# The first two-chunk group's hidden layer in 26 products, its weight sums by accumulating transfers, and block decays made on chip

## The chip, the cores and the metric

The kernel runs on one core of one Trainium2 chip. The metric is the device time of one execution in microseconds (us). Three runs of the kernel before gave 662.61, 662.81 and 662.85; their median, 662.81, is the time that a change is held against. The engines are TensorE (PE, with its weight loads shown apart as PEld), VectorE (DVE), ScalarE (ACT), GpSimd (POOL) and SyncE (SP, which here only issues transfers).

## The reference

Two blocks follow each other: a retention layer with decay, and a two-layer network with the gate h * erf(softplus(h)).

```python
# q, k, v: batch 4, 8 heads, 768 positions, 64 wide, float32
state = gamma[None, :, None, None] * state + np.einsum('bhd,bhe->bhde', k[:, :, t], v[:, :, t])
y[:, :, t] = scale * np.einsum('bhd,bhde->bhe', q[:, :, t], state)
...
x = attn_out.transpose(0, 2, 1, 3).reshape(B * S, H * D)      # 3072 tokens x 512
h = x @ w_in                                                  # w_in 512 x 2048, float64 as given
sp = np.maximum(h, 0.0) + np.log1p(np.exp(-np.abs(h)))
out = ((h * erf(sp)) @ w_out).astype(np.float32)              # w_out 2048 x 512, float64 as given
```

## The kernel before

The sequence is worked through in 24 pieces of 128 positions (`j`), the network in groups (`g`). The first 512 tokens are done plainly: groups 0 to 3 are four quarters of the hidden width (`hidden`, L860 and L878), each followed by the gate on ACT (`gate`, L817 and L830: softplus and erf over 128x2048) and a product with DVE (`gated`, L849), and by the second layer `project` (L896), which sums in four PSUM banks `o0` to `o3` over all four groups. From group 4 on (named `G0`) a group is 256 tokens by half of the hidden width, `s` = (g - G0) % 2 telling which half. There `hidden_steps` computes the layer with 26 block products instead of 32: `STEPS` lists for each product the combined weight block, the combined input block, one of four PSUM banks, and into which blocks of `h` the result is added or subtracted. A first addition to a block of `h` is a copy on ACT (L965, L967), all later ones are additions on DVE (L963). The combined inputs come from `x_sums` (18 DVE subtractions and additions of 128x128, L933), the combined weights from 30 sums of 128x256 blocks of `w_in_sb`, `W_SUMS`, by `sum_in` (L344 on DVE). The second layer of these groups is `project_part` (L1034), seven products instead of eight; three of them stand in the stream of the next group's `hidden_steps`, behind steps 14, 18 and 24. Its combined weights, T1 to T4 for each half, are made by `sums`: a negating copy on ACT (L352) and an accumulating transfer inside the on-chip memory issued by POOL (L353).

The order of instructions on every engine is the order in which the program writes them; no scheduler moves them. An engine that waits holds all that is queued behind it. `waiting`, `pace` and `need` only choose where the weight conversions are written among the other work. The weights come as 64-bit floats and are made 32-bit in 16 pieces by five DVE operations (L313 to L331) and one on ACT (L314) each; `place` says which of four spare areas a piece is loaded into, and `load_pieces_after` loads a later piece when an earlier one in the same area is used up.

Before the change the first half-width group, G0, doesn't use `STEPS`: its weight blocks are not yet summed. `hidden_plain` (L980, copies L983) does its 32 products of 128x128 by 128x256, in two runs with `sub_begin` (scores of the next piece of the sequence) between them. On DVE, in the order of the program, stand around it: `sum_in(1, 12)`, `prepared(j)` (scaling and transposing the next piece, L537 to L550), `gated(3)`, `sum_in(1, 20)`, `x_sums(G0)`, and the rest of the sums of half 1; the sums of half 0 follow before and inside group G0+1. Half 1 is summed first since group G0 + 1 needs it first.

At the very start PE runs `keep_warm` (L495, products of the identity matrix, each two instructions) until the first scaled keys are there (`ret_scale`, L514) and can be transposed (`ret_transpose`, L524). The decay factors of the keys in the layout of the later pieces, `kq_b` and `by_b`, are loaded by SP during group 2 in 17 small transfers (`load_block_scales`, L469 and L473); `block_scales` (L476 to L480) makes the other factors of them on DVE and POOL.

Of the kernel before, what the change touches and what calls it, by code (L numbers as in the profile page):

```python
# [19 lines left out]
P = 128  # L20
C = 128
TCH = 512
FG = 4
# [23 lines left out]
    (16, 2, 6, "+"),  # L47
    (17, 8, 10, "-"),
    (4, 4, 17, "+"),
    (10, 10, 16, "+"),  # L50
    (18, 16, 4, "-"),
# [3 lines left out]
    (21, 9, 20, "+"),  # L55
# [4 lines left out]
    (24, 20, 12, "-"),  # L60
    (25, 18, 7, "+"),
    (2, 2, 3, "+"),
    (8, 12, 8, "-"),
    (12, 17, 12, "-"),
# [3 lines left out]
    (16, 16, 7, "+"),  # L68
# [7 lines left out]
    (13, 13, 7, "-"),  # L76
)
# [28 lines left out]
    (24, (0, 1), 1, False, ((7, False),)),  # L106
    (25, 15, 2, False, ((2, True),)),
# [4 lines left out]
    (17, 1, 3, True, ((2, False), (4, True))),  # L112
# [7 lines left out]
    (16, 12, 1, False, ((3, True),)),  # L120
# [16 lines left out]
def kernel(  # L137
# [87 lines left out]
    def w_in_of(ft, kk):  # L225
        half, s, i = ft // (2 * FG), ft % (2 * FG) // FG, ft % FG
        return w_in_sb[:, s, 4 * (2 * half + i // 2) + kk, i % 2 * P : (i % 2 + 1) * P]

    def w_out_of(ft):
        half, s, i = ft // (2 * FG), ft % (2 * FG) // FG, ft % FG  # L230
        return w_out_sb[:, s, 2 * half : 2 * half + 2, i, :]
# [14 lines left out]
    last_power = halves(spare[1][:, :CE])  # L246
# [7 lines left out]
    place = [n % 4 if n < n_p - 4 else (n - n_p + 4) % 3 for n in range(n_p)]  # L254
# [30 lines left out]
    def conversion(n):  # L285
# [4 lines left out]
        half, s, at = i // 4, i % 4 // 2, i % 2  # L290
# [49 lines left out]
    def sum_in(s, upto):  # L340

        assert all(("hidden", 2 * FG + s * FG + u) in done for u in range(FG))
        for to, a, b, sign in W_SUMS[in_sums[s] : upto]:
            nc.vector.tensor_tensor(w_in_sb[:, s, to], w_in_sb[:, s, a], w_in_sb[:, s, b], op=OP[sign])  # L344
        in_sums[s] = max(in_sums[s], upto)

    def sums(s):

        assert ("project", s) in done
        x = {name: w_out_sb[:, s, at] for name, at in OUT.items()}  # L350
        for to, a, b in (("T1", "12", "11"), ("T2", "22", "T1"), ("T3", "22", "12"), ("T4", "21", "T2")):
            nc.scalar.activation(x[to], x[b], AF.Copy, scale=-1.0)  # L352
            nc.gpsimd.dma_start(x[to], x[a], accum_op=ALU.add)  # L353
            done.add((to, s))
            yield
# [47 lines left out]
    nc.scalar.copy(idle_out, ident[:, :1])  # L403

# [60 lines left out]
    def load_block_scales():  # L465
        for s, d in itertools.product(range(2), range(2)):
            part = slice((2 * s + d) * 32, (2 * s + d + 1) * 32)
            for u in range(HP):
                nc.sync.dma_start(  # L469
                    kq_b[part, 0, 0, u],  # L470
                    decay_k[:, 2 * u + s : 2 * u + s + 1].rearrange("(a p) h -> p (a h)", p=32),
                )
        nc.sync.dma_start(by_b[:, 1], decay_s)  # L473
# [13 lines left out]

    psum_turn = itertools.cycle((ps_r, ps_h))
# [8 lines left out]
    keep_warm(7)  # L497
# [68 lines left out]
    def ret_mask(j):  # L566
        AM[j] = ret.tile([P, 2, HP, C], F32, name="am")
        for s in range(2):
            nc.vector.tensor_tensor(
                AM[j][:, s], SC[j][s], causal[:, None, :].to_broadcast([P, HP, C]), op=ALU.mult  # L570
            )
        pace(-1.2)
# [59 lines left out]
    def sub_mask(j):  # L632
        AM[j] = ret.tile([P, 2, HP, C], F32, name="am")
        for s in range(2):
            nc.vector.tensor_tensor(
                AM[j][:, s, :, :D],
                SC[j][s][:, :, :D],
                causal_d[:, None, :].to_broadcast([P, HP, D]),
                op=ALU.mult,
            )  # L640
# [26 lines left out]
    def sub_results(j):  # L667
# [15 lines left out]
        for crossed in range(2):  # L683
            for u in PAIRS:
                for a in range(2):
                    r = 1 - a if crossed else a
                    col, t = u // 2, slice(a * D, (a + 1) * D)
                    own = slice(col * D, (col + 1) * D)
                    nc.tensor.matmul(
                        pp[a][own, 2 + u % 2, :D] if crossed else pp[a][own, u % 2, t],  # L690
                        V[j][t, 2 * u + r, :],
                        AM[j][t, r, u, :D],
                        start=False, stop=True, skip_group_check=True,
                    )
# [18 lines left out]
    def sub_visit(j, g):  # L713
# [31 lines left out]
        def of_values(crossed):  # L745
            for u in PAIRS:
                for a in range(2):
                    r = 1 - a if crossed else a
                    col, t = u // 2, slice(a * D, (a + 1) * D)
                    own = slice(col * D, (col + 1) * D)  # L750
                    nc.tensor.matmul(  # L751
                        other[a][own, u % 2, D:] if crossed else pp[a][own, u % 2, t],
                        V[j][t, 2 * u + r, :],
                        AM[j][t, r, u, :D],
                        start=crossed or first(r, col), stop=True, skip_group_check=True,
                    )
# [108 lines left out]
    def hidden(g, u):  # L865
# [14 lines left out]
        if ft == FG - 1:  # L880
            need("in", FG + 2)
        if g:
            pace_around(3.4 if ft > FG else 0)

    def project(g, tt):
# [17 lines left out]
        if step == TT - 1:  # L903
            done.add(("project", g))
        pace_around(3.4)
# [64 lines left out]

    def hidden_plain(g):

        m, s = chunk_of(g), (g - G0) % 2
        HS[g] = act.tile([P, N], F32, name="h")
        h = HS[g].rearrange("p (f t u c) -> p f u t c", f=2, t=2, u=FG)
        x = XC[m // 2][:, :, m % 2 * SCH : (m % 2 + 1) * SCH]
        for f, u in itertools.product(range(2), range(FG)):
            to = ps_h.tile([P, TCH], F32, name="hp")[:, :SCH]
            for kk in range(n_k):
                nc.tensor.matmul(  # L980
                    to, w_in_of((2 * f + s) * FG + u, kk), x[:, kk], start=kk == 0, stop=kk == n_k - 1
                )
            nc.scalar.copy(h[:, f, u], to.rearrange("p (t c) -> p t c", t=2))  # L983
            yield
        done.update(("hidden", (2 * f + s) * FG + u) for f in range(2) for u in range(FG))
# [164 lines left out]

    for g in range(G0):
# [10 lines left out]
        if g:  # L1162
            for tt in range(TT):
# [3 lines left out]
                elif g == 2 and tt == 0:  # L1167
                    sub_results(4)
                    sub_begin(5, ps_h)
                    load_block_scales()  # L1170
# [16 lines left out]
    sum_in(1, 12)  # L1187
# [3 lines left out]
    for n, _ in enumerate(hidden_plain(G0), start=1):  # L1191
        if n in (1, 4, 7):
            next(last_steps)
        if n == 3:
            sub_begin(j)
    sum_in(1, 20)
    x_sums(G0)
    sub_states(j)
    all_of(prepared(j + 1))
    sum_in(1, len(W_SUMS))  # L1200
    project(G0 - 1, 0)
    nc.scalar.activation(idle, idle, AF.Softplus)
    gate_softplus(G0)
    sub_visit(j, G0)
    load(j + 3)
    put_first(0)
    gate_erf(G0)
    next(last_steps)
    sum_in(0, 12)
    for tt in range(1, TT):  # L1210
# [3 lines left out]
    sum_in(0, 20)  # L1214
    j += 1

    def sums_left():
        for n in range(21, len(W_SUMS) + 1):
            sum_in(0, n)
# [4 lines left out]
    for g in range(G0 + 1, NG):  # L1224
# [15 lines left out]
        if g == G0 + 1:  # L1240
            order.update({n: (w_sums,) for n in (1, 2, 3, 4)})
            for n in (14, 16, 18, 20, 24):
                order[n] += (w_sums,)
# [16 lines left out]
        all_of(w_sums)  # L1260
# [89 lines left out]
```

## Time and profile before

| | |
|---|---|
| median of three runs | 662.81 us |
| span of the profiled execution, first to last instruction | 660.9 us (its whole time isn't given apart) |
| PE busy, share of the span | 655.7 us, 99% |
| DVE, ACT, POOL busy | 508.4, 280.2, 11.7 us |
| group 3's second layer for group 2 ends, `hidden_plain` begins | 127.6 us |
| `hidden_steps` of G0+1 begins | 158.4 us |
| DVE ends the last conversion | 116.6 us |

The profile is of one execution. A row of groups gives the line, engine, operation, tiles written and read, shapes, count, busy time and mean length of one, and the idle time before it. A row in order of time gives the start in us from the span's start, the length, and the group; in square brackets stands the engine's idle time before it and what ended it. Matmuls overlap, so their cost in a stream is the distance from start to start. One 32-bit product is two PE instructions.

### The profile page before, as it was taken

The numbers are of one execution on the slowest core, as the hardware profiler recorded it, in microseconds if no ns is written. First come the engines' busy times: TensorE is split into PE (matmuls) and PEld (weight loads), VectorE is DVE, ScalarE is ACT, GpSimd is POOL, SyncE is SP. The second block draws the span as 40 slices with busy tenths as digits, with TensorE's granted clock in tenths as the row PEclk, the third lists the DMA queues.
The fourth block names the chain that finished last, engine by engine and source line by source line (L and its number), as shares of the span: only waits on it lengthen the run. The fifth ranks groups of instructions, "written<-read, shape, count | busy, mean of one in ns | idle before, by whom it ended". The sixth has DMA issues, their size and how long they took to land.

```text
span 660.9 us, 15247 instructions
## 1 busy us (share of the span) xinstructions
PE 655.7 (99%) x6200; PEld 557.3 (84%) x6200; DVE 508.4 (77%) x1102; ACT 280.2 (42%) x402; POOL 11.7 (2%) x29
## 2 busy tenths in 40 slices
PE   8999999999999999999999999999999999999998
PEld 7744444576999999999999999999999999999997
DVE  5999999969986786788678678677687688476464
ACT  3468363445534334244254253342432542533440
POOL 1000000110100000000000000000000000000000
PEclk9999999999999999999999999999999999999999
DMA  9999844385753321222222322221231210000000
GB/s 188 223 264 231 211 129 107 63 152 90 144 123 61 85 47 32 67 47 46 70 44 47 73 39 46 42 72 37 44 79 36 46 53 1 2 34 0 1 33 32
DMA packets 159413, 51.88 MB, mean 78 GB/s; under 512 B 143216, under 2 KB 149744, under 8 KB 159344
## 3 DMA queue, kind: packets, MB, share of 16 engines
q1 hardware_dynamic: 157776, 46.72, 32.8%
q0 software_dynamic: 1152, 4.19, 3.4%
q8 instruction: 48, 0.79, 0.5%
q14 instruction: 21, 0.17, 0.1%
q10 hardware_dynamic: 416, 0.01, 0.0%
HBM read 40.39 MB, written 6.29 MB: 71 GB/s over the span
## 4 chain that ended last, share of the span: by engine, by line
PE 98%; DMA 1%; DVE 0%; ACT 0%; issue 0%
PE o L1034 37%; PE hp L951 22%; PE r L951 12%; PE hp L860 8%; PE o L896 8%; PE hp L980 2%; PE r L736 2%; PE hp L628 1%; PE o L772 1%; PE r L524 1%; PE r L557 1%; PE o L604 1%; PE r L751 1%; PE hp L751 1%; DMA kq<-in_k_dram 1%; PE r L772 0%
## 5 line engine op out<-in xcount | busy, mean ns | idle before, releaser
L1034 PE MATMUL o<-w_out_sb,h 128*128 128x256 f32 (+1 forms) x640 | 142.7, 380 | 0.0
L951 PE MATMUL hp<-xs,w_in_sb 128*128 128x128 f32 x988 | 138.1, 275 | 0.0
L1034 PEld LDWEIGHTS o<-w_out_sb,h 128*128 128x128 f32 x640 | 119.5, 190 | 16.6
L963 DVE TENSOR_TENSOR h<-h,hp 128x256 f32<-128x256 f32 x190 | 78.0, 418 | 70.5 <-PE hp L951 65.6
L951 PEld LDWEIGHTS hp<-xs,w_in_sb 128*128 128x128 f32 x988 | 128.4, 192 | 3.0
L1034 PE MATMUL o<-w_out_sb,e 128*128 128x256 f32 x480 | 113.5, 379 | 0.0
L1034 PEld LDWEIGHTS o<-w_out_sb,e 128*128 128x128 f32 x480 | 86.8, 190 | 9.4
L817 ACT ACTIVATE e<-h 128x2048 f32<-128x2048 f32 x22 | 42.1, 1912 | 119.6 <-DVE h L963 119.6
L963 DVE TENSOR_TENSOR h<-h,r 128x256 f32<-128x256 f32 x152 | 56.9, 415 | 22.3 <-PE r L951 21.4
L965 ACT COPY h<-hp 128x256 f32<-128x256 f32 x38 | 14.2, 373 | 130.7 <-PE hp L951 122.7
L951 PE MATMUL r<-xs,w_in_sb 128*128 128x128 f32 x456 | 63.3, 275 | 0.0
L951 PEld LDWEIGHTS r<-xs,w_in_sb 128*128 128x128 f32 x456 | 57.0, 192 | 0.0
L860 PE MATMUL hp<-xT,w_in_sb 128*128 128x512 f32 (+2 forms) x144 | 56.5, 548 | 0.0
L849 DVE TENSOR_TENSOR e<-h,e 128x1024 f32<-128x1024 f32 x42 | 49.2, 1213 | 8.0 <-ACT e L830 8.0
L860 PEld LDWEIGHTS hp<-xT,w_in_sb 128*128 128x128 f32 x144 | 25.8, 190 | 27.0 <-issue 24.6
L951 PE MATMUL hp<-xT,w_in_sb 128*128 128x128 f32 x304 | 46.3, 275 | 0.0
L951 PEld LDWEIGHTS hp<-xT,w_in_sb 128*128 128x128 f32 x304 | 41.5, 192 | 1.4 <-issue 0.5
L830 ACT ACTIVATE e<-e 128x2048 f32<-128x2048 f32 (+1 forms) x23 | 42.1, 1836 | 0.2
L967 ACT ACTIVATE h<-hp 128x256 f32<-128x256 f32 x57 | 21.9, 384 | 29.7 <-PE hp L951 28.3
L951 PE MATMUL r<-xT,w_in_sb 128*128 128x128 f32 x228 | 31.7, 275 | 0.0
L830 ACT ACT_TABLE_LOAD x24 | 30.8, 1283 | 0.4
L951 PEld LDWEIGHTS r<-xT,w_in_sb 128*128 128x128 f32 x228 | 28.5, 192 | 0.0
(164 smaller groups left out, 799.0 us busy)
## 6 DMA issues: line engine op xcount, KB each, us to landing
w_out_sb<-in_moe_w_out_dram SPq DMA_DIRECT2D x14, 512.0 KB, 5.2
kq<-in_k_dram SPq DMA_DIRECT2D x23, 256.0 KB, 4.0
v<-in_v_dram SPq DMA_DIRECT2D x23, 256.0 KB, 3.4
out_dram<-r SPq DMA_DIRECT2D x23, 256.0 KB, 2.9
kq<-in_q_dram SPq DMA_DIRECT2D x288, 16.0 KB, 1.9
kb<-in_k_dram SPq DMA_DIRECT2D x288, 16.0 KB, 1.8
w_in_sb<-in_moe_w_in_dram SPq DMA_DIRECT2D x8, 512.0 KB, 10.1
w_out_sb<-w_out_sb POOLq DMA_DIRECT2D x8, 512.0 KB, 5.3
```

What stands on the lines that cost most here:

```text
L736: nc.tensor.matmul(pp[r][col * D : (col + 1) * D, u % 2, t], x[own, u, :], QT[j][own, u, t], start=first(r, col), stop=True, skip_group_ch ...
L751: nc.tensor.matmul(other[a][own, u % 2, D:] if crossed else pp[a][own, u % 2, t], V[j][t, 2 * u + r, :], AM[j][t, r, u, :D], start=crossed ...
L817: nc.scalar.activation(E[g], HS[g], AF.Softplus)
L830: nc.scalar.activation(E[g][:, half], E[g][:, half], AF.Erf)
L849: nc.vector.tensor_tensor(E[g][:, half], HS[g][:, half], E[g][:, half], op=ALU.mult)
L860: nc.tensor.matmul(HP_[ft][:, t], w_in_of(ft, kk), XC[0][:, kk, t], start=(kk == 0), stop=(kk == n_k - 1),)
L896: nc.tensor.matmul(O[0][tt].rearrange("p (d c) -> p d c", d=2), E[g][:, u * TCH + tt * P : u * TCH + (tt + 1) * P], w_out_of(ft), start=(f ...
L951: nc.tensor.matmul(to[:, u, :], w_in_sb[:, s, w, u * P : (u + 1) * P], XS[m](x), start=first and u == 0, stop=True, skip_group_check=True,)
L963: nc.vector.tensor_tensor(h, h, of, op=ALU.add if plus else ALU.subtract)
L965: nc.scalar.copy(h, of)
L967: nc.scalar.activation(h, of, AF.Copy, scale=-1.0)
L1034: nc.tensor.matmul(O[m][i][:, half, at], G[g][a][:, u * P : (u + 1) * P], w_out_sb[:, s, OUT[b], u, at], start=i not in started, stop=(s = ...
```

## The change

1. G0 uses `hidden_steps` as all later groups do, and `hidden_plain` goes. `sub_begin` comes behind the layer, two parts of `project` for group 3 follow before `sub_visit`, and `x_sums(G0)` goes ahead of `prepared`.
2. For this the numbering of hidden-width quarters changes (`w_in_of`, `w_out_of`): groups 0 and 1 now use the weights of half 0, groups 2 and 3 those of half 1. Half 0 is therefore free for summing after group 1.
3. The 30 sums of half 0 become `MOVES`: 20 entries taken one by one in `hidden` (for groups 2 and 3) and in `project` (for groups 0 to 2). An entry copies blocks on ACT (20 copies in all, some negated) and adds one block or two at once by an accumulating transfer that POOL issues (19 issues in the order of instructions on POOL). One sum, `last_sum`, stays on DVE behind step 5 of G0's layer. Half 1 is summed on DVE as before, seven sums between the steps of G0's layer, then 13, then one behind each of the first ten steps of G0+1.
4. One of the four spare areas for weight pieces lies in blocks that the new sums use, so the later pieces use three (`place`); piece 11 is loaded when piece 8 is used up, where it was piece 7.
5. `load_block_scales` goes. A matrix of copied identity columns (`spread`, made by POOL) is multiplied with the key decays at the start: four products with eight columns on PE, two copies on ACT, two small ones on POOL. Two of the seven first `keep_warm` products go.
6. The masked scores of the first pieces use a buffer of `act`, and those of the later ones become half as large.

```diff
+MOVES = (
+    ((("n0", 6, -1), ("n1", 10, -1), (24, 8, 1)), (((4, 24), "n"),)),
+    (((8, 8, -1),), (((1, 8), (5, 12)),)),
+    (((25, 2, 1),), (((7, 25), (3, 6)),)),
+    ((), ()),
+    ((), ()),
+    (((12, 12, -1),), (((4, 10), (24, 25)),)),
...
+    (((15, 15, -1), ("n0", 2, -1)), (((17, 19), (18, 18)), ((6,), "n"))),
+    ((), (((16, 21), (20, 20)), ((7,), (10,)))),
+    ((), (((6, 13), (14, 23)),)),
+    ((), (((3,), (15,)), ((6,), (12,)))),
+    ((), (((15,), (2,)),)),
+)
...
-        half, s, i = ft // (2 * FG), ft % (2 * FG) // FG, ft % FG
+        s, half, i = ft // (2 * FG), ft % (2 * FG) // FG, ft % FG
...
-    place = [n % 4 if n < n_p - 4 else (n - n_p + 4) % 3 for n in range(n_p)]
+    place = (0, 1, 2, 3, 0, 1, 2, 3, 0, 1, 2, 0, 1, 2, 0, 1)
...
+    def moved_sums():
...
+        for copies, adds in MOVES:
+            for to, of, sign in copies:
...
+                if sign > 0:
+                    nc.scalar.copy(block(to), block(of))
+                else:
+                    nc.scalar.activation(block(to), block(of), AF.Copy, scale=-1.0)
+            for to, of in adds:
+                src = block("n0") if of == "n" and len(to) == 1 else blocks(of)
+                nc.gpsimd.dma_start(blocks(to), src, accum_op=ALU.add)
+            yield
+
+    def last_sum():
+        assert next(moves, 0) == 0
+        nc.vector.tensor_tensor(
+            w_in_sb[:, 0, 13], w_in_sb[:, 0, 13], w_in_sb[:, 0, 7], op=ALU.subtract
+        )
...
+    spread = w_in_sb[:, 1, 24:26].rearrange("p x (b f) -> p (x b) f", f=P)
+    nc.gpsimd.tensor_copy(
+        spread.rearrange("p a (g f) -> p a g f", f=32),
+        ident.rearrange("p (a o f) -> p a o f", a=4, o=1).to_broadcast([P, 4, 4, 32]),
+    )
...
-    def load_block_scales():
-        for s, d in itertools.product(range(2), range(2)):
...
+    def spread_scales():
...
+        for r in range(2):
+            own = slice(r * D, (r + 1) * D)
+            nc.gpsimd.tensor_copy(by_b[own, 1], d_s[own, r])
+        x = ps_o.tile([P, 4, H], F32, name="o1")
+        for a in range(4):
+            nc.tensor.matmul(x[:, a], spread[:, a], d_k, start=True, stop=True)
+        for r in range(2):
+            own = slice(r * D, (r + 1) * D)
+            nc.scalar.copy(
+                kq_b[own, 0, 0], x[own].rearrange("p a (u s) -> p s u a", s=2)[:, r]
+            )
...
-    keep_warm(7)
+    keep_warm(5)
+    spread_scales()
...
+        if g > 1:
+            next(moves, None)
...
+        if g + 1 < G0:
+            next(moves, None)
...
-    sum_in(1, 12)
+    x_sums(G0)
     all_of(prepared(j))
     load(j + 2)
     gated(G0 - 1)
-    for n, _ in enumerate(hidden_plain(G0), start=1):
-        if n in (1, 4, 7):
+    for n, _ in enumerate(hidden_steps(G0), start=1):
+        if n == 5:
+            last_sum()
+        if n in (11, 17, 23):
             next(last_steps)
-        if n == 3:
-            sub_begin(j)
-    sum_in(1, 20)
-    x_sums(G0)
+        if n >= 8 and n % 3 == 2:
+            sum_in(1, n // 3 - 1)
+    sub_begin(j)
+    project(G0 - 1, 0)
     sub_states(j)
     all_of(prepared(j + 1))
-    sum_in(1, len(W_SUMS))
-    project(G0 - 1, 0)
+    sum_in(1, 10)
     nc.scalar.activation(idle, idle, AF.Softplus)
     gate_softplus(G0)
+    project(G0 - 1, 1)
     sub_visit(j, G0)
     load(j + 3)
     put_first(0)
+    put_first(1)
     gate_erf(G0)
     next(last_steps)
-    sum_in(0, 12)
-    for tt in range(1, TT):
+    sum_in(1, 20)
+    for tt in range(2, TT):
         project(G0 - 1, tt)
         put_first(tt)
     gated(G0)
-    sum_in(0, 20)
...
         if g == G0 + 1:
-            order.update({n: (w_sums,) for n in (1, 2, 3, 4)})
-            for n in (14, 16, 18, 20, 24):
-                order[n] += (w_sums,)
+            order.update({n: (w_sums,) for n in range(1, 10)})
+            order[10] += (w_sums,)
```

## The prediction

> **What bounds the kernel now.** I read the page's busy times first, then the chain of work that ended last, then the groups by shape, then the time-ordered rows around the place of the change.
>
> ```profile
> PE 655.7 (99%) x6200; PEld 557.3 (84%) x6200; DVE 508.4 (77%) x1102; ACT 280.2 (42%) x402; POOL 11.7 (2%) x29
> ...
> PE 98%; DMA 1%; DVE 0%; ACT 0%; issue 0%
> ```
>
> TensorE (PE) is busy for 655.7 of 660.9 us and is 98% of the chain. What is left is 1.46 us before its first matmul, 2.8 us after its last, and three waits of 0.2 to 0.3 us before 15 us. So an edit moves the time only by what it does to PE's own queue: work taken off it, work put on it, and new waits in it. The groups by shape and PE's rows in order of time give the prices:
>
> ```profile
> L980 PE MATMUL hp<-xT,w_in_sb 128*128 128x256 f32 x64 | 14.2, 381 | 0.0
> ```
>
> ```profile
> 127.60 5.34 PE L980 MATMUL hp<-xT,w_in_sb 128*128 128x256 f32 x24
> 132.87 0.69 PE L628 MATMUL r<-qT,kT 64*64 64x64 f32 x32
> 133.39 0.64 PE L648 MATMUL r<-v,kq 64*64 64x64 f32 x16
> 133.96 8.90 PE L980 MATMUL hp<-xT,w_in_sb 128*128 128x256 f32 x40
> 142.70 3.60 PE L896 MATMUL o<-w_out_sb,r 128*128 128x512 f32 x8
> ...
> 162.87 1.06 PE L951 MATMUL r<-xs,w_in_sb 128*128 128x128 f32 x8
> 163.76 1.06 PE L951 MATMUL hp<-xs,w_in_sb 128*128 128x128 f32 x8
> 164.66 1.89 PE L1034 MATMUL o<-w_out_sb,e 128*128 128x256 f32 x8
> ```
>
> Columns: start, length, then the group. The mean of one (381 ns) overlaps its neighbours; what counts is start to start. G0's plain layer fills 127.60 to 142.70 except 1.09 us for `sub_begin`: **14.01 us** (32 products, two instructions each, 64 in all). The 26-product form of the next group takes 0.89 us for eight instructions, which is two steps of `STEPS`: 0.447 us a step.
>
> **Part by part. PE's work at G0.** Removed: 14.01 us. Added: 26 steps by 0.447 = 11.61 us. On work alone: -2.40 us. `sub_begin` only moves behind the layer.
>
> **New waits inside those 26 steps.** This is where I choose. In the groups G0+1 and later, `project_part` stands on PE behind steps 14, 18 and 24, 1.73 us each (164.66 to 166.38). In G0's layer nothing stands there. Two steps take a PSUM bank that the vector engine (DVE) must still read: step 15 (bank 0, read after step 13) and step 25 (bank 0, read after step 24). The last group shows how late such a read is, and an early wait how soon PE goes on:
>
> ```profile
> 637.97 0.61 PE L951 MATMUL hp<-xs,w_in_sb 128*128 128x128 f32 x4
> 638.41 0.61 PE L951 MATMUL hp<-xT,w_in_sb 128*128 128x128 f32 x4
> 638.61 0.87 DVE L963 TENSOR_TENSOR h<-h,hp 128x256 f32<-128x256 f32 x2 [0.55 <-PE hp L951]
> ```
>
> ```profile
> 14.42 0.42 DVE L806 COPY state<-o 128x256 f32<-128x256 f32 x1 [0.61 <-ACT xT L618]
> ...
> 14.89 0.67 PE L597 MATMUL o<-qT,state 64*64 64x128 f32 x16 [0.34 <-DVE state L806]
> ```
>
> A read starts 0.64 us after its step (637.97 to 638.61), takes 0.42, and PE restarts 0.05 after it (14.84 to 14.89); after a wait the next matmul comes 0.1 later than in a stream (8.30 to 8.52 where 0.11 is usual). Step 25: 0.64 + 0.42 + 0.05 + 0.10 - 0.447 = **0.76 us** of waiting. Step 15 has a step between, so 0.32 if DVE were free; but steps 11 and 12 bring four reads and one weight sum just before (0.335 us each in a row, a sum 0.36). Walked through from the layer's start: step 11 at 4.47, its reads from 5.11, the sum, step 12's reads, and step 13's read from 6.81 to 7.23; PE goes on at 7.38 instead of 6.25: **1.12 us**. Bounds: 0.3 to 1.2 at step 15, 0 to 0.85 at step 25, 0 being the case that neither is held. I take 1.88 in all, since it follows row by row. Behind the waiting matmuls all of PE queues, so it is paid in full: 11.61 + 1.88 = 13.49, against 14.01: **-0.52**.
>
> **DVE around it.** DVE loses 29 of 60 weight sums (0.38 us each, 22.9 us for 60), but PE did not wait for them. In time order DVE ended the weight conversions at 116.64, made 12 sums, `prepared`, and the gating of group 3:
>
> ```profile
> 117.07 4.98 DVE L344 TENSOR_TENSOR w_in_sb<-w_in_sb 128x256 f32<-128x256 f32 x12
> 121.98 0.68 DVE L537 TENSOR_TENSOR kq<-kq,kq_s 128x512 f32<-128x512 f32 x1
> ...
> 125.00 2.31 DVE L849 TENSOR_TENSOR r<-h,r 128x1024 f32<-128x1024 f32 x2
> ```
>
> Now the 18 `x_sums` stand first (130.31 to 134.52 in the old order: 4.2 us), so they end near 121.3, and PE wants the first at 128.05: covered. The gating ends near 126.5, and DVE's lateness reaches PE only if it passes 130.6 (step 9 would wait for step 5's read). Cover 4.1 us. What eats it: piece 11 (in7) is now loaded behind piece 8, at 77.4 instead of 70.3; such loads landed in 6.6 to 11.7 us and DVE wants it at 85.6 (0 to 3.5 us); and two of the 20 new ScalarE (ACT) copies stand ahead of a conversion that DVE waits for at 91.2 (0.75 us). Together about 1 to 2.5 us: nothing reaches PE. In group G0+1 ten sums instead of four come in the first ten steps, and step 15 there comes **0.2 us** late by the same walk (bounds 0 and 0.8).
>
> **The 19 accumulating transfers** are in no queue of PE's. ACT pays 20 copies of some 0.37 us (7.4 us between 64 and 115 us, where it is idle half the time; the PSUM copies of the hidden layer stand ahead of them in the queue). GpSimd (POOL) pays 19 issues of 0.86 us or a little more, as the eight L353 transfers cost (512 KB each, landed 4.6 to 7.1 us later; these are at most half as large). Waits queue: `(6,13)+=` stands behind `kq_b` on POOL, which waits for DVE's scales (117 to 119) and takes 1.95: issued near 121, landed near 125 to 128; DVE wants it for `last_sum` at 130.4 and PE block 15 (the last transfer, near 130) at 133.0. Cover 2 to 3 us. Cost taken: 0; bounds 0 and +3.
>
> On that, the DMA page of the Trainium skill ("DMA: Bandwidth & Descriptors", section SWDGE vs HWDGE vs iDMA) says that GpSimd writes the descriptors into SBUF, out of which DVE's two-port mode locks it. The transfers now lie beside the conversions, where the eight of the trace did not. By that rule issues could stretch, and only the last three have little cover.
>
> **Decays on chip.** SP loses 17 issues (88.36 to 97.58), after which it waited until 98.3 for DVE anyway; so no load starts earlier and nothing is won. POOL's copies at the start run beside PE's first matmuls. PE gives 4 instructions of warming (0.21 each, 0.85) for 8 with eight columns; these end before 5.05, when DVE's first scaled keys release L524 at 5.11, if one costs under 0.18; 0.21 each would delay by 0.25. Taken: 0.
>
> **Sum.** -0.52 + 0.2 = -0.3 us. The span was 660.9 and the median 662.81, 1.9 us more for what lies around it and taken as constant: span 660.6, time **662.5**.
>
> **Rivals.** (1) *The waits at steps 15 and 25 don't come or are short*: the whole 2.4 us arrives, 660.4. For it: no group in the trace shows PE waiting for DVE; against: each has `project_part` in exactly those places. (2) *Slower: the clock opens one step later.* The first matmuls run at half rate:
>
> ```profile
> 1.46 3.36 PE L495 MATMUL o<-ident 128*128 128x128 f32 x14 [1.46 <-POOL ident masks.py:199]
> 5.11 1.12 PE L524 MATMUL r<-ident,kq 128*128 128x128 f32 x4 [0.29 <-DVE kq L514]
> 6.02 1.06 PE L495 MATMUL o<-ident 128*128 128x128 f32 x4
> 6.87 0.68 PE L524 MATMUL hp<-ident,kq 128*128 128x128 f32 x4
> ```
>
> L495 has 0.213 us start to start up to 6.87 and 0.11 after, 5.4 us from the first matmul. (The granted clock in the rows is 1.00 all along, so the rate is read from the spacing.) The change thins the work from 3.6 (ten instructions) to 5.1. If the count starts again at 5.11 and needs the same 5.4 us, the half rate lasts to 10.5, 3.6 us longer: 17 instructions at 0.21 instead of 0.11 cost 1.7, so 664.2. It decides if PE's rows after 6.87 still stand 0.21 apart. The skill's "TensorE: Matmul & The Clock Gate", Part 1, calls this a gate that opens after one busy window of about 3.4 us; by it the new, thinner window may not count as busy, and the price would be one window at half rate. (3) *DVE or a transfer is late at G0*: beyond 4.1 us of lateness each us costs one; +1 to +4, 663.5 to 666.5. (4) *The 26 products use weights that aren't there in time at the first step*: the same price, counted in (3).
>
> **How the numbers follow.** Forecast 53% (661.9 to 663.2), (1) 17%, (2) 22%, (3) 8%. 0.2% is 1.33 us, about what a measurement of this kernel can tell from no change: faster is below 661.48, all of (1); slower above 664.14, some 0.13 of (2) and 0.06 of (3). Range 660.4 to 664.6: it takes in (1) and the middle of (2).
>
> **What would show it.** PE rows of G0's layer: 26 steps in about 13.5 us, with gaps before steps 15 and 25 put down to DVE's `h` (right), or 11.6 without gaps (rival 1). The first 10 us: 0.11 spacing from about 6.9, or from 10. No idle before the layer's first step, and DVE's `last_sum` not waiting for DMA. I am wrong if PE waits anywhere between 15 us and the layer, or if the layer's waits exceed 2.4 us.

## The result and the profile after

The changed kernel took **682.59 us** (median of four runs, 681.09 to 688.52), the kernel before 662.83 beside it: a ratio, worked out from all runs and not from the medians, of 1.0314 with a 95% interval of 1.0288 to 1.034; by the medians **19.8 us slower** where the forecast was 0.3 faster. The profiled execution took 681.71, with a span of 680.0 against 660.9: 19.1 us to be found in the trace.

A piece of the sequence is called a chunk from here on, to keep it apart from the pieces of the weights; the visit is `sub_visit`, where PE takes up the next chunk.

Of the page, the busy times, the slices of PE and of its granted clock, and the chain:

```profile
PE 661.3 (97%) x6244; PEld 560.6 (82%) x6244; DVE 504.7 (74%) x1091; ACT 286.5 (42%) x424; POOL 34.0 (5%) x51
...
PE   8999679998999999999999999999999999999998
...
PEclk9999799998999999999999999999999999999999
...
PE 83%; DVE 6%; issue 4%; DMA 4%; SPq 3%; ACT 1%; POOL 0%; DVEq 0%; POOLq 0%; ACTq 0%
```

A slice is 17 us. PE is not full in the slices from 68 to 102 us, long before the layer that was changed, and its clock falls to 0.7 in one of them. The chain, 98% PE before, now runs for a sixth of the span through other things. PE's waits (us in total, times, longest):

```profile
PE hp L933 <- DVE w_in_sb L354: 5.7, 1, 5.7
PE hp L1028 <- DVE h L1040: 2.4, 3, 1.0
PE o L971 <- DVE w_out_sb L354: 2.3, 1, 2.3
PE hp L701 <- DVE qT L623: 2.0, 1, 2.0
...
PE hp L933 <- ACT w_in_sb L396: 1.3, 1, 1.3
```

Only the second line holds waits that the prediction worked out, two of its three; the third of them, 0.99 us, is in the layer of G0+3. The first and third lines are weights that DVE had not converted, the fourth the next keys and queries. The fifth the trace puts down to one of the new copies on ACT, which stood behind a step of a late conversion and two PSUM copies. DVE's rows in order of time (start, length, operation; in brackets the idle time before and what ended it):

```profile
61.31 1.23 DVE L345 SCALAR_TENSOR_TENSOR w_out_sb<-w_out_sb,w_in_sb 128x1024 f32<-128x1024 uint32 x1
70.98 0.69 DVE L336 TENSOR_SCALAR xs<-w_in_sb 128x1024 uint32<-128x1024 uint32 x1 [8.45 <-DMA w_in_sb<-negated]
...
75.31 1.22 DVE L587 TENSOR_TENSOR kq<-kq,kq_s 128x1024 f32<-128x1024 f32 x1
81.57 0.69 DVE L340 TENSOR_SCALAR w_out_sb<-w_in_sb 128x1024 uint32<-128x1024 uint32 x1 [5.04 <-DMA w_in_sb<-w_in_sb]
```

Before, the same two steps stood in a stretch in which DVE had no idle time at all:

```profile
61.15 0.69 DVE L313 TENSOR_SCALAR xs<-w_in_sb 128x1024 uint32<-128x1024 uint32 x1
...
66.61 0.68 DVE L317 TENSOR_SCALAR w_out_sb<-w_in_sb 128x1024 uint32<-128x1024 uint32 x1
```

Now DVE stands still for 8.45 and 5.04 us. Both times it is about to read the raw words of weight piece 7, and both times what lets it go is an *accumulating transfer*: `(4,24) += negated`, landed at 70.95, and `(7,25) += (3,6)`, landed at 81.47. Piece 7's words lie in blocks 16 to 23, and no transfer writes these. But each of the two is one transfer into two blocks, and the stretch from the first block to the second, 4 to 24 and 7 to 25, reaches across 16 to 23.

PE's row after the wait, and the stretch that holds most of it (busy time and instructions of PE, PEld, DVE, ACT and POOL, granted clock, DMA share, GB/s):

```profile
75.45 9.95 PE L933 MATMUL hp<-xT,w_in_sb 128*128 128x512 f32 x16 [5.73 <-DVE w_in_sb L354]
```

```profile
76.00:84.00 8.00, 8.00 (x14) 3.22 (x13) 2.92 (x4) 0.00 (x0) 1.20 (x1) 0.68 0.71 121
```

Sixteen of these matmuls take some 7.0 us in a stream (24 take 10.46 before); here 9.95, at a mean clock of 0.68. So this idle time of 5.73 us costs about 3 us more behind it.

The account, by how much later than before a mark in PE's rows comes (three experiments, told below, are set beside it):

| PE's mark | before, us | changed | e1 | f1 | k1 |
|---|---|---|---|---|---|
| group 0's main stream | 27.27 | +1.26 | +1.01 | +1.75 | 0.00 |
| G0's layer begins | 127.60 | +14.18 | +1.01 | +1.75 | +0.89 |
| G0+1's layer begins | 158.41 | +17.59 | +3.34 | +1.49 | -1.01 |
| G0+4's layer begins | 236.16 | +19.01 | +8.83 | +2.64 | +0.19 |
| span | 660.9 | +19.1 | +8.9 | +2.7 | +0.3 |

G0's layer itself did what was worked out: 13.66 us to `sub_begin`, forecast 13.49, with its two waits at steps 15 and 25 (in brackets the idle time; counted from start to start, with the slower restart, they cost 1.17 and 0.78):

```profile
149.10 0.71 PE L1028 MATMUL hp<-xs,w_in_sb 128*128 128x128 f32 x4 [0.90 <-DVE h L1040]
...
154.35 0.71 PE L1028 MATMUL hp<-xs,w_in_sb 128*128 128x128 f32 x4 [0.51 <-DVE h L1040]
```

### The profile page after: what moved, and what is told of

It reads as the page before. It is cut to its first block, busy times and chain, and to the rows that moved or that the text cites. A ratio compares the mean times of both kernels' runs of the same rounds, so it can differ in the third digit from the quotient of the medians.

```text
span 680.0 us, 15400 instructions
## 1 busy us (share of the span) xinstructions
PE 661.3 (97%) x6244; PEld 560.6 (82%) x6244; DVE 504.7 (74%) x1091; ACT 286.5 (42%) x424; POOL 34.0 (5%) x51
## 4 chain that ended last, share of the span: by engine, by line
PE 83%; DVE 6%; issue 4%; DMA 4%; SPq 3%; ACT 1%; POOL 0%; DVEq 0%; POOLq 0%; ACTq 0%
PE o L1095 35%; PE hp L1028 21%; PE r L1028 11%; PE o L971 5%; SPq L210 2%; PE hp L933 2%; DMA w_in_sb<-in_moe_w_in_dram 2%; PE r L809 1%; PE hp L701 1%; DMA w_in_sb<-w_in_sb 1%; PE o L845 1%; DVE w_out_sb L345 1%; DVE xs L348 1%; DMA w_in_sb<-negated 1%; DVE w_out_sb L340 1%
## 5 line engine op out<-in xcount | busy, mean ns | idle before, releaser
L1028 PE MATMUL hp<-xs,w_in_sb 128*128 128x128 f32 x1040 | 145.8, 275 | 2.4 <-DVE h L1040 2.4
L1028 PEld LDWEIGHTS hp<-xs,w_in_sb 128*128 128x128 f32 x1040 | 134.9, 192 | 6.2 <-DVE h L1040 3.3
L1040 DVE TENSOR_TENSOR h<-h,hp 128x256 f32<-128x256 f32 x200 | 82.1, 419 | 71.6 <-PE hp L1028 66.8
L1040 DVE TENSOR_TENSOR h<-h,r 128x256 f32<-128x256 f32 x160 | 60.1, 417 | 21.8 <-PE r L1028 21.0
L1028 PE MATMUL r<-xs,w_in_sb 128*128 128x128 f32 x480 | 66.7, 275 | 0.0
L933 PE MATMUL hp<-xT,w_in_sb 128*128 128x512 f32 (+2 forms) x144 | 59.7, 570 | 7.0 <-DVE w_in_sb L354 5.7
L1028 PEld LDWEIGHTS r<-xs,w_in_sb 128*128 128x128 f32 x480 | 60.0, 192 | 0.0
L933 PEld LDWEIGHTS hp<-xT,w_in_sb 128*128 128x128 f32 x144 | 26.7, 198 | 36.4 <-issue 25.4
L1028 PE MATMUL hp<-xT,w_in_sb 128*128 128x128 f32 x320 | 48.8, 275 | 0.0
L1028 PEld LDWEIGHTS hp<-xT,w_in_sb 128*128 128x128 f32 x320 | 43.7, 192 | 1.9 <-issue 1.0
L971 PE MATMUL o<-w_out_sb,r 128*128 128x512 f32 x64 | 29.5, 612 | 2.3 <-DVE w_out_sb L354 2.3
```

Source lines behind the costliest of these rows:

```text
L933: nc.tensor.matmul(HP_[ft][:, t], w_in_of(ft, kk), XC[0][:, kk, t], start=(kk == 0), stop=(kk == n_k - 1),)
L971: nc.tensor.matmul(O[0][tt].rearrange("p (d c) -> p d c", d=2), E[g][:, u * TCH + tt * P : u * TCH + (tt + 1) * P], w_out_of(ft), start=(f ...
L1028: nc.tensor.matmul(to[:, u, :], w_in_sb[:, s, w, u * P : (u + 1) * P], XS[m](x), start=first and u == 0, stop=True, skip_group_check=True,)
L1040: nc.vector.tensor_tensor(h, h, of, op=ALU.add if plus else ALU.subtract)
```

## The experiments

Theory A: a *false wait*. Two-block transfers hold up the conversion of a piece that lies between their blocks. Rival B: the transfers, or the copies ahead of them, are too slow for this place. Each result stands against the kernel before on the same chip. A profile shows one execution, and the kernels with waits spread widely: g3's six runs lie between 672.57 and 678.74, k2's six between 664.36 and 668.76.

| kernel | median, us | ratio to before (95%) |
|---|---|---|
| e1 pairs split | 671.28 | 1.0113 (1.0088 to 1.0139) |
| e2 first pair split | 678.74 | 1.0253 (1.0227 to 1.0279) |
| e3 transfers held back | 674.45 | 1.0180 (1.0165 to 1.0195) |
| e4 before, with decays on chip | 664.04 | 1.0021 (1.0011 to 1.0030) |
| f1 e1 without transfers | 664.83 | 1.0023 (1.0013 to 1.0033) |
| f2 e1, chunk 6 begun early | 669.04 | 1.0091 (1.0064 to 1.0118) |
| f3 e1, decays later | 670.75 | 1.0115 (1.0099 to 1.0131) |
| f4 f2 and f3, with cover | 671.72 | 1.0124 (1.0092 to 1.0157) |
| g1 sums on GpSimd | 675.45 | 1.0201 (1.0184 to 1.0218) |
| g2 g1, decays later | 674.00 | 1.0162 (1.0149 to 1.0175) |
| g3 g2, with cover | 676.47 | 1.0201 (1.0175 to 1.0226) |
| h1 before, with transfers | 675.83 | 1.0194 (1.0164 to 1.0224) |
| i1 e1, key blocks on GpSimd's queue | 673.47 | 1.0156 (1.0136 to 1.0175) |
| i2 i1, decays later, cover | 672.29 | 1.0138 (1.0121 to 1.0155) |
| i3 e1, chunk 7's on ScalarE's queue | 673.79 | 1.0172 (1.0157 to 1.0187) |
| i4 i3, decays later, cover | 672.03 | 1.0134 (1.0121 to 1.0148) |
| k1 e1, chunk 7's on GpSimd's queue, decays later, cover | **662.16** | **0.9992 (0.9984 to 1.0001)** |
| k2 k1 with half of them there | 667.18 | 1.0064 (1.0045 to 1.0083) |

### e1: the pairs split

```diff
-    ((("n0", 6, -1), ("n1", 10, -1), (24, 8, 1)), (((4, 24), "n"),)),
+    ((("n0", 6, -1), ("n1", 10, -1), (24, 8, 1)), (((4,), "n0"), ((24,), "n1"))),
-    (((25, 2, 1),), (((7, 25), (3, 6)),)),
+    (((25, 2, 1),), (((7,), (3,)), ((25,), (6,)))),
```

> The changed kernel with the two transfers (4,24) += negated and (7,25) += (3,6) each made as two transfers of one block. Theory A (a false wait: piece 7's raw words lie in blocks 16 to 23, which no transfer writes, but the strided pairs 4..24 and 7..25 reach across them, so VectorE's conversion of piece 7 waits for both transfers to land): the 8.45 and 5.04 us of VectorE's idle time at 71 and 81 us go, and with them TensorE's waits of 5.73, 1.27, 2.33 and 1.99 us and the halved clock behind them; 662.83 + 1.26 (start) - 0.35 (G0's layer) = 663.7, within 662.8 to 664.8. Rival B (the transfers themselves, or ScalarE's copies ahead of them, are too slow for this place): more transfers of the same bytes help nothing, over 676.

671.28. The same bytes go to the same blocks, and DVE's waits are gone (its rows):

```profile
62.16 0.69 DVE L336 TENSOR_SCALAR xs<-w_in_sb 128x1024 uint32<-128x1024 uint32 x1
...
67.61 0.69 DVE L340 TENSOR_SCALAR w_out_sb<-w_in_sb 128x1024 uint32<-128x1024 uint32 x1
```

G0's layer begins 1.01 us late instead of 14.18. Theory A holds, for 11.3 us of the median, and for these waits B falls. But 8.6 us are left where 0.9 was expected. They come behind the layer: PE waits 2.36 us for `qT` of chunk 7 at the visit of G0, and 3.6 us in the layer of G0+3. Behind both DVE waits for a load:

```profile
151.36 0.69 DVE L620 TENSOR_TENSOR kb<-kb,kq_b 128x512 f32<-128x512 f32 x1 [6.22 <-DMA kb<-in_k_dram]
```

The last transfer of chunk 7 lands at 151.7, before at 139.6. Hence theory A2: the transfers take the DMA engines' time from the loads of the chunks, on which SP works without a break from 102 us on.

### e2 and e3: one pair, and the pairs held back

e2 splits only the first row above. e3 splits nothing:

```diff
+            if ("in", 11) in done:
+                for _ in range(1 + (held > 0)):
+                    next(steps, None)
+                held = max(held - 1, 0)
+            else:
+                held += 1
```

> Only the first of the two pairs is split, (7,25) += (3,6) stays a pair. Theory A: the wait of 8.45 us goes, but the second step of piece 7's conversion still waits for the pair to land. It is issued behind ScalarE's gate at about 68 us and takes some 8 us, so VectorE resumes near 76 instead of 82 us: between the split kernel and the changed one, about 672 (667 to 678). Theory B: as the changed kernel, over 676. If the first pair alone is the cause: near 664.

> Nothing is split: the pairs stay, but the first rows of the transfers are held back until piece 7 has been converted, and then issued two rows at a time. Theory A: the cure is the same as with the split, 662.8 to 665.5, with a little more lateness at the later rows. Theory B (the transfers are slow, or there is too little time for them): later issue makes it worse, over 680. If pairs cost more than single blocks by themselves, it lies well above the split kernel.

e2: 678.74, just above its range, and by the time alone as B has it (over 676). The rows tell them apart: the wait at L336 is gone, the one at L340 stays, as it should by A, and is longer, since DVE comes to it sooner:

```profile
77.46 0.69 DVE L340 TENSOR_SCALAR w_out_sb<-w_in_sb 128x1024 uint32<-128x1024 uint32 x1 [9.84 <-DMA w_in_sb<-w_in_sb]
```

e3: 674.45, with whole pairs and no wait of DVE at piece 7. Its time is neither A's nor B's (over 680); later issue should have made it worse than the changed kernel by B. It misses A's range by what e1 misses, and by 3 us more: PE waits 3.0 us for DVE's `xT` at 107 and 2.6 at the visit.

### e4 and f3: the start

e4 is the kernel before with `spread_scales` for `load_block_scales` and 5 warming products for 7. f3 is e1 with 7, and the products later:

```diff
-    keep_warm(5)
-    spread_scales()
+    keep_warm(7)
...
-        [([], [])] * FG,
+        [([], []), ([], []), ([(spread_scales,)], []), ([], [])],
```

> The kernel before, with only the key decays of the blocks made on chip at the start (5 warming products in place of 7, then 4 products of 8 columns) in place of the 33 small transfers. Theory A: the whole delay of the start comes from these, +1.26 us: 664.1 (663.6 to 664.6), with TensorE at half rate until about 8.4 us instead of 6.9. Rival: the delay of the start comes from elsewhere in the change (order of loads, other pools): 662.8, no change.

> The split kernel with 7 warming products at the start as before, and the four small products that spread the decays moved to the third hidden tile of group 0, where TensorE runs at full rate. Theory A: the start's 1.26 us go and nothing is paid for it, 671.3 - 1.2 = 670.1 (669.4 to 670.6). Rival: these products cost as much wherever they stand (their 8 weight loads and products): 671.3.

e4: 664.04, 1.3 us over before: the start's delay is the decays'. (The small transfers that it does without are 17, not 33.) PE's rows in e4:

```profile
3.76 1.75 PE L479 MATMUL o<-d_k,w_in_sb 128*128 128x8 f32 x8
5.36 1.09 PE L536 MATMUL r<-ident,kq 128*128 128x128 f32 x4
```

The eight instructions take 0.2 us each, as much as a warming product of 128 columns, and end past 5.11, when the first transposes could have begun. The spacing of 0.21 then lasts to 8.8 instead of 6.87. The moment differs between executions: f1, with the same start, still has it at 9.34, and its main stream begins 0.74 us later than e1's. f3: 670.75, within 0.6 us of e1 and of the spread of both: inconclusive by time. By its rows the main stream begins at 27.48 instead of 28.28, but the products cost 0.81 us where they now stand, at full rate (the next row begins at 36.25):

```profile
35.44 0.95 PE L540 MATMUL r<-d_k,w_in_sb 128*128 128x8 f32 x8
```

So the rival is partly true. The products with 8 columns are bound by their weight loads: in e4 these stand one behind the other without a gap, eight in 1.78 us, as long as eight of the warming products'. With 7 warming products f3 has the full rate at its first transposes, 3.5 us after its first matmul:

```profile
5.00 0.66 PE L597 MATMUL r<-ident,kq 128*128 128x128 f32 x4 [0.19 <-DVE kq L587]
```

### f1 and h1: no transfers, and nothing but transfers

```diff
-                nc.gpsimd.dma_start(blocks(to), src, accum_op=ALU.add)
+                pass
```

```diff
+    def idle_moves():
+        for n in range(19):
+            nc.gpsimd.dma_start(w_in_sb[:, n % 2, 24:26], w_in_sb[:, 0, :2], accum_op=ALU.add)
+            yield
```

> The split kernel without the accumulating transfers into the input weights (the copies ahead of them stay; so the sums of half 0 are not made). Theory A2 (the second loss: the accumulating transfers take the DMA engines' time just when the blocks of chunks 6 and 7 are loaded, so a load takes 22.9 us on SyncE's queue where it took 18.4, and chunk 7 lands 12 us later): loads of 18 us again, TensorE's waits of 2.36 and 3.6 us go, 662.8 + 1.26 - 0.35 = 663.7 (663.0 to 664.8). Rival C (not the transfers, but the new places and order of the weights' pieces, by which SyncE comes to chunk 6 2.6 us later and DVE is late): the waits stay, over 667.

> The kernel before, with 19 accumulating transfers of two adjoining blocks (256 KB each) added at the places where the changed kernel issues its own. They go into blocks 24 and 25, which nothing reads before the sums overwrite them, so that no conversion and no step of TensorE needs their result, and nothing else of the change is there. Theory A2 (their time on the DMA engines alone makes the loads of chunks 6 to 9 late): the load of chunk 6 takes some 22 us on SyncE's queue in place of 18, chunk 7 lands 8 to 10 us later, and TensorE gets waits of some microseconds at the visits and layers behind it: 664.5 to 669. Rival (transfers hurt only by what waits for them, or by the change's other order of the weights): within 1 us of the kernel before, 662.0 to 663.8.

f1 leaves out the sums of half 0, so it doesn't compute the network, and only its time counts: 664.83, at the upper end of A2's range, 6.5 us under e1; of the two waits, 0.7 us is left, at G0+3. Chunk 6 occupies SP's queue for 22.9 us in e1, 19.6 in f1, 18.5 before; chunk 7 for 22.8, 18.8 and 18.0 (from its first issue to that of chunk 8; SP's rows in e1, then f1):

```profile
124.88 0.63 SPq L228 DMA_DIRECT2D kq<-in_k_dram  x1
...
147.71 0.85 SPq L228 DMA_DIRECT2D kq<-in_k_dram  x1
```

```profile
122.13 0.53 SPq L228 DMA_DIRECT2D kq<-in_k_dram  x1
...
140.93 0.58 SPq L228 DMA_DIRECT2D kq<-in_k_dram  x1
```

SP comes to chunk 6 some 3 us later than before in f1 as in e1: that is C's part, and it costs little.

h1: 675.83, 12.9 us over before, more than expected, though nobody awaits these transfers. Only the one before the last held each of them back, so 17 of the 19 ran from 27 to 104 us, and most landed 6 to 11 us after issue. Loads came late one after the other, and DVE for them (us in total, times, longest), and PE with waits of 4.5, 3.0 and 2.2 us:

```profile
DVE kb L551 <- DMA kb<-in_k_dram: 12.4, 3, 9.0
```

As they ran at other times, 12.9 us is no measure of their price in the changed kernel.

### f2 and f4: chunk 6 begun early, and cover for the layer's waits

```diff
         [
-            ([], []),
+            ([(load_begin, 6)], []),
...
+        if n in (14, 24):
+            project(G0 - 1, 0, slice(2) if n == 14 else slice(2, 4))
     sub_begin(j)
-    project(G0 - 1, 0)
+    project(G0 - 1, 1)
```

> The split kernel, with the keys and the query blocks of chunk 6 (17 of its 34 transfers) issued at the first hidden tile of group 2, where SyncE's queue is idle from 65.3 to 78.4 us. Theory A2: every later load comes some 10 us earlier, the waits of 2.36 and 3.6 us go, 663.7 to 665. Rival D (the DMA engines are already full at 60 to 80 us, 0.88 busy): the loads of the weights' pieces 10 and 11 come later, VectorE's conversions behind them too, nothing is gained: 669 or more.

> All three cures (pairs split, chunk 6 begun early, decays spread later) and two halves of the output product of group 3 put behind steps 14 and 24 of G0's layer, to cover the waits of 0.90 and 0.51 us. If the ledger is complete: 662.8 - 0.35 - 1.4 = 661.1 (660.4 to 662.2). If the loads stay late (rival D): 667 or more.

f2: 669.04, rival D's figure. The waits of 2.36 and 3.6 went, but the query blocks took SP 17.4 us where 13 were free, piece 11's load stood behind them, DVE waited 4.5 us for it and PE 2.3. f4: 671.72, the same twice over (piece 11 late by 10.6 us). Its layer shows the cover at work:

```profile
142.70 1.88 PE L984 MATMUL o<-w_out_sb,r 128*128 128x512 f32 x4
...
168.78 0.71 PE L1041 MATMUL hp<-xs,w_in_sb 128*128 128x128 f32 x4 [1.78 <-ACT h L1055]
```

The layer takes 15.14 us with eight output instructions in it (3.43), so 11.71 without: no wait at steps 15 and 25. The second row gives most of it back. Those products had covered ACT's copies and `erf` behind the layer; now G0+1's fifth step waits for ACT. From here on only two quarters (four instructions) are moved.

### g1 to g3: the sums on GpSimd

```diff
-                nc.gpsimd.dma_start(blocks(to), src, accum_op=ALU.add)
...
+                    nc.gpsimd.tensor_tensor(x[:, to], x[:, a], x[:, b], op=OP[sign])
```

> The changed kernel with the sums of half 0 made by GpSimd, block by block, in place of ScalarE's copies and the accumulating transfers (the layer in 26 steps and the start stay as changed). Theory A and A2 (the false wait and the DMA engines' time are the only large losses): both are gone, 662.8 + 1.26 - 0.35 = 663.7 (663.0 to 664.8), loads of 18 us. Rival E (VectorE and GpSimd hinder each other: VectorE is 98% busy from 60 to 130 us, so every slower conversion lands on TensorE): over 666.

> The kernel with GpSimd's sums, with 7 warming products at the start and the decays' products moved to the third hidden tile of group 0. Theory A: 1.2 us under the kernel with GpSimd's sums, 662.5 (661.9 to 663.4). Rival: the products cost the same there: no difference.

> The same with two quarters of the first output product of group 3 behind steps 14 and 24 of G0's layer, 0.9 us of TensorE's work each. If the two waits of 0.90 and 0.51 us are what keeps the layer from gaining: 1.4 us under the kernel without them, 661.1 (660.5 to 662.2). Rival: the layer's later steps then wait for VectorE all the same, as its sums are behind: under 0.5 us gained.

g1: 675.45, rival E. The loads of chunks 6 and 7 take 19 us again, but DVE's rows grow while GpSimd works (74 to 109 us):

```profile
79.53 1.74 DVE L345 SCALAR_TENSOR_TENSOR w_out_sb<-w_out_sb 128x1024 f32<-128x1024 uint32 x1
81.19 1.22 DVE L336 TENSOR_SCALAR xs<-w_out_sb 128x1024 uint32<-128x1024 uint32 x1
```

1.22 and 0.69 elsewhere. PE waits 5.2 us for the output weights. The Trainium skill's "SBUF — State Buffer", section Who interferes with whom, says that a VectorE instruction with two SBUF inputs, or in a two-port mode, contends with a GpSimd instruction that reads SBUF, so that one blocks the other; these rows agree. g2 is 1.5 us under g1, as the start would have it. g3's cover gains 1.6 us from G0's layer to G0+1's, as expected, and gives it back: chunk 9 is 7.7 us late for DVE, and PE waits 4.4 us at G0+3. Neither theory had that. In this kernel what G0 gains is lost at the loads.

### i1 to i4, k1, k2: the queue, or the engines' time?

In f1 the DMA engines were 0.21 to 0.52 busy during a load, chunk 6's, that still took 19.6 us, one issue of 0.5 to 0.7 us after another. So A2 has a rival of its own: not the engines' time is short, but *one queue* without slack, which the transfers stretch.

```diff
-            load_blocks(KB[j], k[b, :, now, :])
+            if j == JPC + 2:
+                load_blocks(KB[j], k[b, :, now, :])
+            elif j > JPC + 3:
+                load_blocks(KB[j], k[b, :, now, :])
...
+    load_blocks(KB[JPC + 3], k[(JPC + 3) // NC, :, (JPC + 3) % NC * C : ((JPC + 3) % NC + 1) * C, :], nc.gpsimd)
     x_sums(G0)
```

That is k1's, with `load_blocks` issuing on the queue it is given; i1 and i2 also put chunks 8 and 9 there, i3 and i4 use `nc.scalar`, k2 moves 8 of the 16.

> The split kernel, with the 16 key blocks of chunks 7, 8 and 9 issued on GpSimd's queue (chunk 7's behind the last accumulating transfer, near 129 us) instead of SyncE's. In the kernel without transfers the DMA engines were 0.21 to 0.52 busy during such a load and it still took 18.8 us: 34 issues of some 0.5 us one after another. If SyncE's queue, one transfer after another, is what the accumulating transfers stretch and what has no slack, two queues in parallel bring chunks 7 to 9 some 8 us sooner, and the waits of 2.36 and 3.6 us go: 664 to 665.5, with the transfers still there. If the DMA engines' time itself is short, the blocks land as late from either queue: 669 or more.

> The same with the decays' products in the third hidden tile of group 0 (0.4 us gained over all, by the rows of f3) and two quarters of an output product behind steps 14 and 24 of G0's layer (1.6 us gained at the layer in g3). If the loads are no longer late: 2 us under the kernel with two queues, 662 to 663.5, level with the kernel before. If earlier work at G0 only meets the next load: no more than 0.5 us under it.

> The split kernel with the 16 key blocks of chunk 7 alone issued on ScalarE's queue, where ScalarE is idle from 122.7 to 129.3 us, and every other load on SyncE's. On GpSimd's queue the loads came in time (no wait at the visit of G0, none at G0+3), but the transfers of the output weights' sums stood behind them, ScalarE waited 15.6 us for the first, and TensorE 4.3 us for ScalarE. If the second loss is one of queues, chunks 7 to 9 are now in time and nothing stands behind them: 663.7 to 665.5. If the DMA engines' time is short: 668 or more. If 16 issues of 0.45 us are too much for ScalarE there, the layer's first copies come late, 1 to 2 us on top.

> The same with the decays' products in group 0 and two quarters of an output product behind steps 14 and 24 of G0's layer: 2 us less (0.4 and 1.6), 661.7 to 663.5, level with the kernel before or a little faster. If earlier work at G0 only meets the next late load or a busy ScalarE, as in g3 and f4: no gain over the kernel without them.

> The split kernel with the decays' products in group 0, the two quarters of an output product in G0's layer, and the key blocks of chunk 7 alone on GpSimd's queue, behind the last accumulating transfer. On ScalarE's queue the 16 issues took 13.2 us and held up its copies (TensorE waited 6.2 us), but no load was late afterwards. On GpSimd's they take 8.7 us (132 to 141), and the first of the output weights' sums comes 6 us later, which ScalarE has room for between the layer and the visit. If queues are the second loss, nothing is late any more: 662 to 664. If the DMA engines' time is short, chunk 7 or 9 stays late: 667 or more.

> The same, with eight of chunk 7's key blocks on GpSimd's queue and eight on SyncE's: the output weights' sums come only 2 us later, chunks 8 and 9 some 4 us later than in the kernel with all sixteen there. If both the sums and the loads have a little room: the same, 662 to 664. If the loads have none, a wait at G0+3 of 1 to 2 us comes back: 664 to 667.

i1 to i4 missed their times, 672 to 674, and were right on the loads: in none of them is there a wait at the visit or at G0+3. What came instead is what now stood behind the moved issues. In i1 it is the transfers of the output weights' sums, in i3 the layer's first copies (rows of ACT in i1, then i3):

```profile
155.04 2.00 ACT L419 ACTIVATE w_out_sb<-w_out_sb 128x1024 f32<-128x1024 f32 x2 [15.58 <-DMA w_out_sb<-w_out_sb]
```

```profile
136.78 0.37 ACT L1046 COPY h<-hp 128x256 f32<-128x256 f32 x1 [13.61 <-DMA kb<-in_k_dram]
```

PE waited 4.3 and 6.2 us for ACT (2.6 and 3.9 in i2, 7.2 in i4). k1 has neither obstacle, and is **662.16, level with the kernel before**, 20 us under the changed one; PE has no wait of over 0.2 us behind 15 us. The transfers are all there, and the engines as busy as in e1 (e1, then k1; the next to last column):

```profile
110.00:120.00 10.00, 10.00 (x24) 4.37 (x23) 9.83 (x16) 6.81 (x9) 7.07 (x7) 1.00 0.90 129
```

```profile
110.00:120.00 10.00, 10.00 (x25) 4.46 (x24) 9.83 (x16) 6.95 (x9) 6.94 (x7) 1.00 0.93 134
```

So the transfers do stretch each load (chunk 6 takes 21.8 us in k1 too), but the loss lies in the one queue that has no room for it: 16 issues out of it, and nothing is late. What is not shown is how the 9.1 us between e1 and k1 divide: k1 also has the later decays and the cover, and no run moves chunk 7's issues to GpSimd's queue without these two. Where the two were added to an otherwise equal kernel they gained 1.2 (i2) and 1.8 us (i4). k2: 667.18, with 1.87 us of waiting at G0+3, as was said for the case that the loads have no room. Its profiled execution took 665.45; what the slower ones waited for isn't on record.

## Why the prediction was wrong, point by point

- **G0's layer, 11.61 of work and 1.88 of waits: right.** 13.66 against 13.49, and the waits cost 1.17 and 0.78 (forecast 1.12 and 0.76) at the steps named; 11.71 where they were covered (f4).
- **"The 19 accumulating transfers are in no queue of PE's ... Cost taken: 0; bounds 0 and +3": this step failed**, in two ways that make 17.8 of the 19.8 us. It asked only who awaits the *results* of the transfers. It did not ask who waits for a transfer that lies *across* its operand (DVE's conversion of piece 7: 11.3 us, e1), nor which queue is stretched by them (SP's loads: 6.5 us, f1, k1). The cover of 2 to 3 us was counted for the last sums, where nothing went wrong. POOL's issues did stretch, most to 1.2 us and more; but in h1 most took 0.86 beside the conversions, so these alone don't account for it, and the loss lay elsewhere.
- **"DVE around it ... Cover 4.1 us ... nothing reaches PE": wrong by the same omission.** DVE ended the conversions at 132.25, where 116.64 stood before. The two items that were counted are small: in e1 the layer begins on time.
- **"no load starts earlier and nothing is won": half right.** That SP's queue has no slack was in the trace of before: loads back to back until 223 us, and DVE waiting 3.18 us for chunk 7 at 139.3. I used it to strike out a gain and not to price a loss.
- **Decays, "Taken: 0": wrong by 1.3 us.** The bound "0.21 each would delay by 0.25" came true for the first transposes (5.36 in e4 for 5.11), but had too low a price, since the full rate came later as well: rival 2, its 1.7 measured as 1.3 (e4). The full rate came 3.4 us after the dense stream began at 5.36 in e4, 3.5 us after the first matmul in f3, but 5.4 us after it in the kernel before. The rule from the Trainium skill's "TensorE: Matmul & The Clock Gate", Part 1, a busy window of about 3.4 us, agrees with these as the least time; it doesn't tell how much later it comes in one execution.
- **Group G0+1, +0.2**: 0.17 in the changed kernel; 1.2 in k1, where it starts 1.0 us sooner, above the bound of 0.8.
- **Rival 3**, DVE or a transfer late, "+1..+4", had the right kind, a fifth of the size, and the wrong place: the first loss came some 60 us before G0, the second behind it.
- **Not foreseen: a wait can cost more than its length**, by PE's clock. Behind 5.73 us of idle time 16 matmuls took 3 us longer. Behind 1.99 us at the visit the work up to G0+1 took 9.28 us where e1 needed 7.83; yet e1 had waited 2.36 us there and its granted clock stayed at 1.00. So the length of the wait alone doesn't decide it, and what does is open.

With nobody held up, the rest of the account stands: k1, which also covers the layer's waits and pays the decays' 0.8 us elsewhere, ends 0.6 us under the kernel before, a difference that its interval doesn't tell from none. Open: whether more can be had, since g3 lost at the loads what it gained at G0; why G0+1's layer took 1.2 us longer in k1; and what a paced copy of the transfers alone costs in the kernel before.

## What to carry to other kernels

Before you move work to a transfer, ask of the profile what lies *between* the blocks that a strided access touches and who uses it meanwhile, and which queue has no slack in that stretch, since every transfer in it gets longer. A queue's slack is the distance from landing to use, not its share of busy time. When you take issues out of one queue, look at what then stands behind them in the other: of three places tried, one was free.

## What the hardware showed that was not expected

- PE's granted clock fell to 0.68 for 8 us after an idle time of 5.73, and to 0.83 over 10 us after one of 1.99 (2.09 in f3); after one of 2.36 (e1) it stayed at 1.00.
- An accumulating transfer of 256 KB within SBUF landed 6 to 11 us after issue beside the loads (h1), and from 80 to 100 us, where four of them were issued and the loads were late, the profile's busy share of the DMA engines was 1.07 for 0.49 before.
- Sixteen small loads (16 KB each) cost ScalarE's queue 13.2 us, GpSimd's 8.7, SyncE's 9 to 12 in the same stretch.
- GpSimd's additions of 128x256 (1.32 us each) made VectorE's operations on 128x1024 longer by 0.5 us.
